# Attention weights times v: three fp32r products of split operands, or whole fp32 with each head on its own columns

## The chip, the cores and the metric

One Trainium2 chip, one of its NeuronCores. The metric is device time of one execution in microseconds (us); times of several runs are given by their median. TensorE (PE), VectorE (DVE), ScalarE (ACT), GpSimd (POOL) and the DMA queues (SP's above all) work side by side and meet at semaphores. The profile is of one execution, and its granted TensorE clock is shown as a share of 2.4 GHz.

## What is computed

Attention with a band and global tokens, then a token-shifted feed-forward layer ("Mix" in the kernel), then a routed layer of eight experts:

```python
k_all = np.concatenate([k_g, k_l], axis=2); v_all = np.concatenate([v_g, v_l], axis=2)
out_g = sm(scale * q_g @ k_all.T) @ v_all            # 32 global queries, 544 keys
mask = np.abs(pos[:, None] - pos[None, :]) <= 32
s_ll = np.where(mask, scale * q_l @ k_l.T, -1e9)     # 512 local queries
a_l = sm(np.concatenate([scale * q_l @ k_g.T, s_ll], axis=-1))
out_l = a_l @ np.concatenate([v_g, v_l], axis=2)
x = concat([out_g, out_l])                           # 4 x 544 x 512
x = _moe_ref(x)                                      # Mix: relu(xk@w_k)^2 @ w_v * sigmoid(xr@w_r)
return _moe2_ref(x)                                  # one expert of 8 for each token
```

Batch 4, 8 heads of 64, all in fp32.

## The kernel before, in words

The program has two stages. Up to about 480 us attention and Mix are interleaved; behind that come the experts, which the change doesn't touch.

Attention is cut into 16 units, one for each pair of heads of each batch element (`divmod(u,4)`). In a unit there are four items of 128 local queries (`item`, L212) and one global item of 2 x 32 queries (`gitem`, L257). An item runs through: scores on PE (`twin`, L197, the two heads on the two halves of the array's rows), mask and minimum on DVE (L222), exp on ACT (L225), scaling on POOL (L231), four transposes on PE (L237), a copy out of PSUM (`split`, L106), the product with v on PE (L245), and the eviction into `xT` on ACT (L249, L250). `xT` holds the attention output, transposed, and is what Mix reads.

Units 0 to 3 are "early" (`NF=4`): their operands stay whole fp32. From unit 4 on each operand is split in a high part in fp32r and the rest, and a product is three: high x high, high x low, low x high (`parts`, L105). For the weights `split` does this with a copy on ACT (L118) and a subtraction on DVE (L120) into `ph` and `plo`; for v `prep_v` (L184) does it on POOL (L191, L193), from one staging tile `vn`, into two half tiles. An early unit reads v from one of the two tiles `ve` as it was loaded. The product for an item takes v as the stationary operand with both heads' 128 columns and the weights of both heads as 256 moving columns; two of the four 64 x 128 blocks of the result are used, and two evictions fetch them.

The order of work comes in two steps. Generators announce each piece with its engine, a duration in us and places of buffers (`op("P",.65,("av",),("ph",),...)`), and `Sched` (L42) runs them against clocks of its own, by priority; the tile framework's scheduler then orders the instructions on each engine by its own timing. Instruction order and DMA order therefore move when a duration or a place count changes. Loads are issued on SP's queue, in order: `load` (L121) for q and k, `load_v` (L134) for v, `weight` (L396) for the weights of Mix, which ACT, DVE and POOL turn into high and low parts (L423 is the last step of each).

Of the kernel before, what the change touches and what calls it, by code (L numbers as in the profile page):

```python
# [34 lines left out]
PP=(0,0,0,1,0,0,0,1); TW=(1,1,1,(2,4,6),3)  # L35
NR=4; NP=4
# [47 lines left out]
class Attn:  # L84


    def __init__(s,tc,ident,mask,q_l,k_l,v_l,q_g,k_g,v_g,xT,sb,ps):
# [4 lines left out]
        s.vn=sb.tile([P,4,2,P],F32,name="vn",bufs=1)
# [7 lines left out]
        s.V={}; s.nat=set(); s.vnat=set(); s.T={}; s.sdone={}; s.vdone={}; s.odone={}  # L100
    def places(s,t):
# [59 lines left out]
    def prep(s,u,name):  # L161
# [21 lines left out]
        s.T[u]["n"]+=1  # L183
    def prep_v(s,u):  # L184
        nc=s.nc; L=[]
        for hf in range(2):
            yield op("G",.59)
            v=s.sb.tile([P,2,2,2,P],F32R,tag=f"v{hf}",name=f"v{u}_{hf}",bufs=1)
            f=lambda a:a.rearrange("p i a c -> p (i a c)")
            i=f(s.vn[:,2*hf:2*hf+2])  # L190
# [21 lines left out]
    def item(s,u,i,S_,held):  # L212
# [34 lines left out]
        yield op("A",.33,(),("av",))  # L247
# [61 lines left out]
    def run(s,sched,units,may):  # L309
        for u in units:  # L310
# [12 lines left out]
    def run_v(s,units):
        for u in units[NF:]:
            yield wait(lambda: u in s.vnat and all(s.vdone.get(v,0)>=5 for v in range(u)))
            yield from s.prep_v(u)

# [784 lines left out]
```

## Time and profile before

| | us |
|---|---|
| median of 3 runs (757.11 to 761.41) | 759.85 |
| the profiled execution's own time | 762.52 |
| its span, first to last instruction | 760.8 |
| PE busy / DVE busy in the span | 707.8 / 481.9 |
| ACT busy / POOL busy in the span | 394.9 / 343.5 |

Busy time of PE is that of its matrix products, which overlap: one lasts about 0.28 us, and the next one can start 0.11 us behind it. So what a group of products costs is read from the starts on the timeline, and a mean duration isn't its price. PEld is the loading of weights, which runs beside the products. A whole fp32 product shows as two records, a transpose or an fp32r product as one. The timeline gives start and duration, engine, source line, tiles out<-in, then rows x columns of the array, partitions x elements of the moving operand, and how many instructions are merged in the row.

### The profile page before, as it was taken

What the parts mean: (1) busy time and instruction counts of PE and PEld (TensorE: products, weight loads), DVE (VectorE), ACT (ScalarE), POOL (GpSimd) and SP (SyncE); (2) the same over time, 40 slices, a digit from 0 to 9 for tenths busy, and PEclk for the clock granted to TensorE, in tenths of its full rate; (3) what the DMA queues carried; (4) which work ended last, traced back from release to release, by engine and by line L of the source; (5) the groups of instructions that cost most, each with busy time, mean ns of one, the idle gap of its engine ahead of it and who ended that gap; (6) DMA issues with size and microseconds to landing.
All of it is one profiled execution on the core that took longest, in us unless ns stands there. A gap on an engine that the chain in (4) does not pass through costs nothing. (4 is left out here: it accounts for less than half of the span.)

```text
span 760.8 us, 13892 instructions
## 1 busy us (share of the span) xinstructions
PE 707.8 (93%) x4702; PEld 606.1 (80%) x4702; DVE 481.9 (63%) x1393; ACT 394.9 (52%) x1038; POOL 343.5 (45%) x483
## 2 busy tenths in 40 slices
PE   4887998899999999999999899989879999999996
PEld 2565786698898988978888789877677999889795
DVE  6587689758697685795864865577844534434361
ACT  4698876754575653565654624324733514335251
POOL 6368858724655246562455262012733513413431
PEclk9899998999999999999999999999989999999999
DMA  6674144211302211202100320225964724606530
GB/s 154 174 223 129 33 121 119 54 30 35 81 17 55 57 23 38 68 22 58 35 21 29 118 104 2 64 103 180 301 226 149 242 85 129 203 26 190 170 126 22
DMA packets 93184, 76.36 MB, mean 100 GB/s; under 512 B 70350, under 2 KB 74446, under 8 KB 93074
## 3 DMA queue, kind: packets, MB, share of 16 engines
q1 hardware_dynamic: 89618, 64.27, 29.0%
q0 software_dynamic: 3456, 10.75, 4.0%
q8 instruction: 53, 0.87, 0.5%
q14 instruction: 57, 0.47, 0.2%
HBM read 66.08 MB, written 9.44 MB: 99 GB/s over the span
## 5 line engine op out<-in xcount | busy, mean ns | idle before, releaser
L231 POOL TENSOR_SCALAR pl<-pl,mx 128x192 f32<-128x192 f32 (+1 forms) x128 | 60.6, 488 | 91.4 <-DVE mx L228 68.8
L21 PE MATMUL psk<-xs,slot0h 128*128 128x256 f32 x256 | 73.4, 290 | 1.8 <-ACT xs L454 1.1
L23 PE MATMUL psk<-xs,slot0h 128*128 128x256 f32 x256 | 73.0, 286 | 0.7 <-POOL xs L456 0.7
L225 ACT ACTIVATE pl<-pl,mx 128x224 f32<-128x224 f32 (+1 forms) x128 | 58.6, 459 | 27.6 <-DVE mx L222 25.7
L24 PE MATMUL psk<-xs,slot0l 128*128 128x256 f32 x256 | 72.1, 282 | 0.0
L900 ACT ACTIVATE hh<-ph 128x256 fp32r<-128x256 f32 (+2 forms) x56 | 22.4, 399 | 78.8 <-PE ph L24 45.6
L456 POOL TENSOR_TENSOR xs<-xm,xs 128x512 fp32r<-128x512 f32 (+1 forms) x36 | 45.7, 1276 | 37.6 <-ACT xs L454 25.5
L449 POOL TENSOR_SCALAR xm<-xT,mut 128x256 f32<-128x256 f32 (+7 forms) x96 | 43.6, 469 | 28.9 <-DVE kl L469 13.1
L21 PE MATMUL psv<-slot1h,kh 128*128 128x512 f32 x136 | 54.9, 404 | 0.3 <-ACT slot1h L421 0.3
L23 PE MATMUL psv<-slot1l,kh 128*128 128x512 f32 x136 | 54.1, 398 | 0.4 <-POOL slot1l L423 0.4
L901 DVE SCALAR_TENSOR_TENSOR hl<-ph,hh 128x256 fp32r<-128x256 f32 (+2 forms) x56 | 24.7, 442 | 46.4 <-ACT hh L900 44.3
L24 PE MATMUL psv<-slot1h,kl 128*128 128x512 f32 x136 | 53.9, 396 | 0.0
L452 DVE SCALAR_TENSOR_TENSOR xm<-xT,mut,xm 128x256 f32<-128x256 f32 (+7 forms) x96 | 47.0, 525 | 6.8 <-POOL xm L449 6.7
L21 PEld LDWEIGHTS psk<-xs,slot0h 128*128 128x128 f32 x256 | 47.8, 189 | 2.8 <-ACT xs L454 1.4
L23 PEld LDWEIGHTS psk<-xs,slot0h 128*128 128x128 f32 x256 | 48.4, 189 | 1.2 <-POOL xs L456 0.9
L24 PEld LDWEIGHTS psk<-xs,slot0l 128*128 128x128 f32 x256 | 48.3, 189 | 0.3
L245 PE MATMUL av<-ph,v 128*128 128x256 f32 x192 | 44.5, 294 | 3.7 <-ACT xT L250 2.6
L872 POOL DMA_INDIRECT xs<-y,idx x23 | 26.7, 1162 | 45.0 <-PE pt L879 22.5
L120 DVE TENSOR_TENSOR plo<-ptp,ph 128x512 fp32r<-128x512 f32 x48 | 32.9, 685 | 18.0 <-ACT ph L118 17.8
L237 PE MATMUL ptp<-ident,pl 128*128 128x128 f32 x256 | 40.3, 283 | 3.2 <-POOL earlyl L176 2.2
L21 PE MATMUL ph<-xh,slot2h 128*128 128x256 f32 (+1 forms) x128 | 38.3, 299 | 5.2 <-issue 5.2
L245 PEld LDWEIGHTS av<-ph,v 128*128 128x128 f32 x192 | 33.2, 191 | 6.6 <-ACT xT L250 3.9
(550 smaller groups left out, 2359.6 us busy)
## 6 DMA issues: line engine op xcount, KB each, us to landing
st<-in_moe_w_dram SPq DMA_DIRECT2D x42, 512.0 KB, 3.9
sw<-in_moe_w_dram SPq DMA_DIRECT2D x22, 512.0 KB, 5.2
y<-r SPq DMA_DIRECT2D x17, 256.0 KB, 2.0
qn<-in_q_l_dram SPq DMA_DIRECT2D x32, 128.0 KB, 4.4
kn<-in_k_l_dram SPq DMA_DIRECT2D x32, 128.0 KB, 2.6
earlyh<-in_moe_w_k_dram SPq DMA_DIRECT2D x8, 512.0 KB
raw<-in_moe_w_v_dram SPq DMA_DIRECT2D x8, 512.0 KB
vn<-in_v_l_dram SPq DMA_DIRECT2D x24, 96.0 KB, 2.0
```

The lines of the kernel that those rows point to most:

```text
L21: i=nc.tensor.matmul(out,wh,xh,start=first,stop=False)
L23: nc.tensor.matmul(out,wh,xl,start=False,stop=False)
L24: return nc.tensor.matmul(out,wl,xh,start=False,stop=last)
L120: nc.vector.tensor_sub(out[1],x,out[0].bitcast(F32))
L225: nc.scalar.activation(p[:,h,ks],p[:,h,ks],AF.Exp,bias=mx[:,h:h+1],scale=-1.0,accum_out=mx[:,4+h:5+h])
L231: nc.gpsimd.tensor_scalar(out=p[:,h,ks],in0=p[:,h,ks],scalar1=mx[:,6+h:7+h],scalar2=0.0,op0=ALU.mult,op1=ALU.add)
L237: nc.tensor.transpose(pt[:,c,h],p[:,h,c*96:c*96+P],s.ident)
L245: nc.tensor.matmul(o,s.v(u,x,i,c),P_[y][:,c],start=c==m==0,stop=c==1 and m==len(parts)-1)
L449: nc.gpsimd.tensor_scalar(out=x[:,u,o:o+k],in0=s.xT[b][:,c,q:q+k],scalar1=m[:,1,c:c+1],scalar2=0.0,op0=ALU.mult,op1=ALU.add)
L452: nc.vector.scalar_tensor_tensor(out=x[:,u,o:o+k],in0=s.xT[b][:,c,1+q:1+q+k],scalar=m[:,0,c:c+1],in1=x[:,u,o:o+k],op0=ALU.mult,op1=ALU.add)
L456: nc.gpsimd.tensor_sub(xl[:,cs,:n],x[:,:,:n],xh[:,cs,:n].bitcast(F32))
L872: s.nc.gpsimd.indirect_dma_start(out=s.xs[i][:,j,:],out_offset=None,in_=s.y,in_offset=IndirectOffsetOnAxis(ap=s.idx[:,ch:ch+1],axis=0))
```

## The change

- Weights and v of all units are whole fp32. `split` has only the copy left for the weights, `prep_v`, `run_v` and the tile `vn` are gone, and the two tiles `ve` serve all units in turn: v of unit u is loaded when the products of unit u-2 are done.
- Each head has a product of its own. For an item the head's 64 columns of v are stationary, its 128 columns of weights move, and the result goes to its own 64 partitions of one PSUM tile, so 64 columns of the array each. That is two chunks x two heads, four products of 64 x 128, and one eviction of 128 x 128 instead of two of 64 x 128.
- For the global item the weights are stationary, 32 columns for each head, and the head's 64 columns of v move: five chunks x two heads, and two evictions instead of one.
- The durations of these pieces are new, `ph` has three buffers instead of two, `plo` is gone.

```diff
-        if s.early(u):
-            vn=s.ve[u%2]
-            yield op("Q",3.5,(),(),lambda: all(s.vdone.get(v,0)>=5 for v in range(u%2,u,2)))
-        else:
-            vn=s.vn
-            yield op("Q",3.5,("vn",))
-            if u==NF: nc.gpsimd.memset(vn,0.0)
+        vn=s.ve[u%2]
+        yield op("Q",3.5,(),(),lambda: all(s.vdone.get(v,0)>=5 for v in range(u%2,u,2)))
...
-    def prep_v(s,u):
-            nc.gpsimd.tensor_scalar(out=f(v[:,0]),in0=i,scalar1=1.0,scalar2=0.0,op0=ALU.mult,op1=ALU.add)
-            nc.gpsimd.tensor_sub(f(v[:,1]),i,f(v[:,0]).bitcast(F32))
...
-        P_=s.weights(u)
-        yield from s.split(u,EV[i],P_,pt.rearrange("p c h q -> p c (h q)"),"pt",(.48,.61))
-        yield op("P",.65 if len(parts)>1 else .87,("av",),("ph",),when=lambda: u in s.V)
-        o=s.ps.tile([P,512],F32,tag="av",name="av",bufs=1)[:,:256]
+        P_=s.weights()
+        yield from s.split(u,EV[i],[P_],pt.rearrange("p c h q -> p c (h q)"),"pt",(.48,.61))
+        yield op("P",.47,("av",),("ph",),when=lambda: u in s.V)
+        o=s.ps.tile([P,512],F32,tag="av",name="av",bufs=1)[:,:P]
         for c in range(2):
-            for m,(x,y) in enumerate(parts):
-                nc.tensor.matmul(o,s.v(u,x,i,c),P_[y][:,c],start=c==m==0,stop=c==1 and m==len(parts)-1)
+            for h in range(2):
+                r=slice(h*HD,(h+1)*HD)
+                nc.tensor.matmul(o[r],s.V[u][:,i,c,r],P_[:,c,h*P:(h+1)*P],start=c==0,stop=c==1)
...
-        nc.scalar.activation(x[0:64,pr,c0:c0+P],o[0:64,0:P],AF.Copy)
-        nc.scalar.activation(x[64:128,pr,c0:c0+P],o[64:128,P:2*P],AF.Copy)
+        nc.scalar.activation(x[:,pr,c0:c0+P],o,AF.Copy)
...
-        yield op("P",.85,("av",),("ph",),when=lambda: u in s.V)
+        yield op("P",.65,("av",),("ph",),when=lambda: u in s.V)
         for c in range(5):
-            cs=slice(c*64,(c+1)*64)
-            for m,(x,y_) in enumerate(parts):
-                nc.tensor.matmul(o,G[x][:,cs],s.v(u,y_,min(c,3),c//4),start=c==m==0,stop=c==4 and m==len(parts)-1)
+            for h in range(2):
+                q=slice(h*32,(h+1)*32)
+                nc.tensor.matmul(o[q],G[:,c*64+h*32:c*64+(h+1)*32],s.V[u][:,min(c,3),c//4,h*HD:(h+1)*HD],start=c==0,stop=c==4)
...
-    sched.add(a.run_v(units),1.5)
```

How this moves instructions, at three places. First PE, at an item of a late unit among the products of Mix (`psl`, `psk`, `psv`; `av` is the value product, `ptp` and `ptq` are transposes, `sga` and `sgb` the global item's scores, a row is one instruction with its output's partitions x columns). Before:

```order
L24 MATMUL psl<-rt,g_250 10x128
L245 MATMUL av<-ph,v_0_3920 128x256
L245 MATMUL av<-plo,v_0_3920 128x256
L245 MATMUL av<-ph,v_0_3920 128x256 x2
L245 MATMUL av<-plo,v_0_3920 128x256
L245 MATMUL av<-ph,v_0_3920 128x256
L237 MATMUL ptp<-ident,pl_115 128x128 x4
```

And after, at a place of the same kind:

```order
L24 MATMUL psv<-slot1h,kl 128x512
L21 MATMUL psv<-slot1h,kh 128x512
L227 MATMUL av<-ph,ve_107 64x128 x4
L242 MATMUL sga<-kw_4279,gT_4280 64x512 x3
L242 MATMUL sgb<-gT_4280 64x32 x3
L160 MATMUL ptq<-ident,qn_4314 128x128 x4
```

Six products over the whole array have become four over 64 columns each, back to back, with full-width work of Mix on either side.

Second POOL, where v of a late unit was split between the scaling of two items (`pl`) and the work on k (`kw`). Before:

```order
L176 TENSOR_SCALAR kw_1752<-gT_1753 128x8x32
L193 TENSOR_TENSOR v_1_1785<-vn,v_1_1785 128x512
L231 TENSOR_SCALAR pl_112<-pl_112,mx 128x192 x2
L231 TENSOR_SCALAR pl_113<-pl_113,mx 128x224 x2
L231 TENSOR_SCALAR pl_114<-pl_114,mx 128x224 x2
L231 TENSOR_SCALAR pl_115<-pl_115,mx 128x192 x2
L191 TENSOR_SCALAR v_0_2040<-vn 128x512
L193 TENSOR_TENSOR v_0_2040<-vn,v_0_2040 128x512
L191 TENSOR_SCALAR v_1_2075<-vn 128x512
L193 TENSOR_TENSOR v_1_2075<-vn,v_1_2075 128x512
```

And after:

```order
L212 TENSOR_SCALAR pl_111<-pl_111,mx 128x192 x2
L212 TENSOR_SCALAR pl_112<-pl_112,mx 128x224 x2
L399 TENSOR_TENSOR slot1l<-w,slot1h 128x512
L169 TENSOR_SCALAR kw_1663<-kw_1663 128x2x3x32 x2
L212 TENSOR_SCALAR pl_113<-pl_113,mx 128x224 x2
L212 TENSOR_SCALAR pl_114<-pl_114,mx 128x192 x2
```

The four steps on v for each late unit are gone from POOL's order; the rest stands as it did.

Third SP's queue in the early part, with what each issue waits for in brackets (DMAHW: a queue's own turn). Loads of `earlyh` are weights of Mix (`w_k`, then `w_r`), `qn`, `kn` and `gn` q, k and the global rows of a unit, `ve` is v. Before:

```order
L406 DMA earlyh<-in_moe_w_k_dram 128x4x256 [waits DMAHW5_49,DVE_49,Activation_49]
L127 DMA qn_417<-in_q_l_dram 128x4x64 [waits DMAHW6_49,PE_49]
L127 DMA qn_417<-in_q_l_dram 128x4x64 [waits DMAHW7_49]
L130 DMA gn<-in_q_g_dram 32x64 [waits DMAHW0_49,PE_49]
L130 DMA gn<-in_q_g_dram 32x64 [waits DMAHW1_49]
L131 DMA gn<-in_k_g_dram 32x2x64 [waits DMAHW2_49]
L146 DMA ve_108<-in_v_l_dram 96x64 [waits DMAHW3_49]
L146 DMA ve_108<-in_v_l_dram 96x64 [waits DMAHW4_49]
L406 DMA earlyh<-in_moe_w_k_dram 128x4x256 [waits DMAHW5_49,DVE_49,Activation_49]
L127 DMA kn_553<-in_k_l_dram 128x4x64 [waits DMAHW6_49,PE_49]
L127 DMA kn_553<-in_k_l_dram 128x4x64 [waits DMAHW7_49]
L406 DMA earlyh<-in_moe_w_k_dram 128x4x256 [waits DMAHW0_49,DVE_49,Activation_49]
```

And after (`qn_591` and `kn_623` belong to unit 4, as `kn_553` does above, and `ve_107` is v of unit 2):

```order
L141 DMA ve_107<-in_v_l_dram 32x4x64 [waits DMAHW2_49,PE_49]
L142 DMA ve_107<-in_v_l_dram 32x3x64 [waits DMAHW3_49]
L143 DMA ve_107<-in_v_g_dram 32x4x64 [waits DMAHW4_49]
L126 DMA qn_591<-in_q_l_dram 128x4x64 [waits DMAHW5_49]
L126 DMA qn_591<-in_q_l_dram 128x4x64 [waits DMAHW6_49]
L126 DMA kn_623<-in_k_l_dram 128x4x64 [waits DMAHW7_49]
L129 DMA gn<-in_q_g_dram 32x64 [waits DMAHW0_49]
L129 DMA gn<-in_q_g_dram 32x64 [waits DMAHW1_49]
L130 DMA gn<-in_k_g_dram 32x2x64 [waits DMAHW2_49]
L382 DMA earlyh<-in_moe_w_k_dram 128x4x256 [waits DMAHW3_49,DVE_49,Activation_49]
L382 DMA earlyh<-in_moe_w_k_dram 128x4x256 [waits DMAHW4_49,DVE_49,Activation_49]
L382 DMA earlyh<-in_moe_w_k_dram 128x4x256 [waits DMAHW5_49,DVE_49,Activation_49]
```

The last three loads of `w_k` stood between the loads of units 3, 2 and 4; now they stand together behind v of unit 2 and all of unit 4's q, k and global rows.

## Rows read from the trace of the kernel before

**Rows 1.** The page, part 1: busy us (share) xinstructions of each engine.
```profile
PE 707.8 (93%) x4702; PEld 606.1 (80%) x4702; DVE 481.9 (63%) x1393; ACT 394.9 (52%) x1038; POOL 343.5 (45%) x483
```

**Rows 2.** Busy time by stage: start:end us, PE, PEld, DVE, ACT, POOL, clock, DMA.
```profile
20.00:100.00 80.00, 69.24 (x433) 52.97 (x434) 57.50 (x191) 63.13 (x209) 53.56 (x82) 0.94 0.51 135
100.00:160.00 60.00, 51.34 (x345) 42.07 (x343) 47.29 (x118) 40.19 (x117) 40.93 (x50) 0.94 0.33 92
160.00:440.00 280.00, 275.36 (x2110) 244.58 (x2109) 204.54 (x717) 160.60 (x486) 130.10 (x215) 1.00 0.18 48
```

**Rows 3.** Timeline of PE: a late global item's products, and a late item's.
```profile
249.43 0.22 PE L290 MATMUL avg<-v,plo 128*64 128x128 f32 x1
...
250.22 0.40 PE L237 MATMUL ptp<-ident,pl 128*128 128x128 f32 x2
...
252.82 0.28 PE L245 MATMUL av<-ph,v 128*128 128x256 f32 x1
...
253.52 0.39 PE L264 MATMUL sga<-kw,gT 128*64 128x512 f32 x1
```

**Rows 4.** Timeline of PE: an early item's products and what follows.
```profile
58.21 1.13 PE L245 MATMUL av<-ph,ve 128*128 128x256 f32 x4 [0.21 <-ACT xT L250]
59.18 0.25 PE L157 MATMUL pgt<-ident,gn 96*128 96x96 f32 x1
```

**Rows 5.** Timeline of PE: an early global item; row three is a narrower window.
```profile
30.58 0.66 PE L167 MATMUL ptq<-ident,kn 128*128 128x128 f32 x4
31.17 1.31 PE L290 MATMUL avg<-ve,ph 128*64 128x128 f32 x10
...
31.98 0.49 PE L290 MATMUL avg<-ve,ph 128*64 128x128 f32 x3
32.41 0.33 PE L167 MATMUL ptq<-ident,qn 128*128 128x128 f32 x1
```

**Rows 6.** Timeline of PE: early scores, the two heads on the array's row halves.
```profile
56.12 0.51 PE L208 MATMUL s__795<-earlyl 64*128 64x192 f32 x2
56.38 0.32 PE L208 MATMUL s__796<-earlyl 64*128 64x192 f32 x1
56.47 0.35 PE L208 MATMUL s__795<-earlyl 64*128 64x224 f32 x1
56.54 0.54 PE L208 MATMUL s__796<-earlyl 64*128 64x224 f32 x2
```

**Rows 7.** Timeline of PE: fp32r products with 64 columns, then full width.
```profile
226.67 0.29 PE L264 MATMUL sgb<-gT 128*64 128x32 f32 x3
226.82 0.37 PE L245 MATMUL av<-ph,v 128*128 128x256 f32 x1
```

**Rows 8.** Groups by line: busy us, mean ns of one; idle before, releasers.
```profile
L120 DVE TENSOR_TENSOR plo<-ptp,ph 128x512 fp32r<-128x512 f32 x48 | 32.9, 685 | 18.0 <-ACT ph L118 17.8
L193 POOL TENSOR_TENSOR v<-vn,v 128x512 fp32r<-128x512 f32 x24 | 32.4, 1351 | 1.1
...
L250 ACT ACTIVATE xT<-av 64x128 f32<-64x128 f32 x64 | 17.5, 273 | 0.8
...
L191 POOL TENSOR_SCALAR v<-vn 128x512 fp32r<-128x512 f32 x24 | 16.3, 678 | 31.7 <-PE av L245 30.8 <-PE pgt L157 0.9
```

**Rows 9.** Waits of PE from 20 to 160 us: total us, times, longest.
```profile
PE av L245 <- ACT xT L250: 3.6, 6, 1.5
...
PE avg L290 <- POOL v L193: 0.6, 1, 0.6
```

**Rows 10.** Timeline of POOL and of PE: last weight conversions, first long uses.
```profile
56.34 1.27 POOL L423 TENSOR_TENSOR slot0l<-w,slot0h 128x512 fp32r<-128x512 f32 x1
...
69.73 1.28 POOL L423 TENSOR_TENSOR wrl<-w,wrh 128x512 fp32r<-128x512 f32 x1
...
91.23 0.60 PE L21 MATMUL psk<-xs,slot0h 128*128 128x256 f32 x3
...
106.75 0.50 PE L21 MATMUL psr<-wrh,xs 128*128 128x512 f32 x1
```

More of the change, by code (lines that the diff above doesn't have):

```diff
@@ L35 @@
 PP=(0,0,0,1,0,0,0,1); TW=(1,1,1,(2,4,6),3)
-NR=4; NP=4
+NR=4; NP=4; NA=3
 FX=(3,5,7); WJ=(288,320,352); MW=352; FW=(2,4,6); NW=(2,3); NST=2
@@ L91, in __init__ @@
         s.gn=sb.tile([96,P],F32,name="gn",bufs=1)
-        s.vn=sb.tile([P,4,2,P],F32,name="vn",bufs=1)
         s.ve=[sb.tile([P,4,2,P],F32,tag=f"v{i}",name=f"ve{i}",bufs=1) for i in range(2)]
@@ L99, in __init__ @@
         nc.gpsimd.memset(s.pg,0.0); nc.gpsimd.memset(s.og,0.0)
-        s.V={}; s.nat=set(); s.vnat=set(); s.T={}; s.sdone={}; s.vdone={}; s.odone={}
+        s.V={}; s.nat=set(); s.T={}; s.sdone={}; s.vdone={}; s.odone={}
     def places(s,t):
@@ L108, in split @@
         nc=s.nc; r=(place,) if place else ()
-        if s.early(u):
+        if s.early(u) or len(out)==1:
             if engine=="A":
@@ L135, in load_v @@
         nc=s.nc; b,pr=divmod(u,4); h0=2*pr
-        if s.early(u):
-            vn=s.ve[u%2]
-            yield op("Q",3.5,(),(),lambda: all(s.vdone.get(v,0)>=5 for v in range(u%2,u,2)))
-        else:
-            vn=s.vn
-            yield op("Q",3.5,("vn",))
-            if u==NF: nc.gpsimd.memset(vn,0.0)
+        vn=s.ve[u%2]
+        yield op("Q",3.5,(),(),lambda: all(s.vdone.get(v,0)>=5 for v in range(u%2,u,2)))
         for j in range(2):
@@ L150, in load_v @@
         yield wait(None)
-        s.vnat.add(u)
-        if s.early(u): s.V[u]=[vn]
+        s.V[u]=vn
     def prep_g(s,u):
@@ L183, in prep @@
         s.T[u]["n"]+=1
-    def prep_v(s,u):
[L185 to L190, printed above, removed]
-            nc.gpsimd.tensor_scalar(out=f(v[:,0]),in0=i,scalar1=1.0,scalar2=0.0,op0=ALU.mult,op1=ALU.add)
-            yield op("G",1.23,(),("vn",) if hf else ())
-            nc.gpsimd.tensor_sub(f(v[:,1]),i,f(v[:,0]).bitcast(F32))
-            L.append(v)
-        s.V[u]=L
     def cols(s,i): return slice(32*(i==0),224-32*(i==3))
@@ L238, in item, with weights @@
         s.pt_.append(p)
-        P_=s.weights(u)
-        yield from s.split(u,EV[i],P_,pt.rearrange("p c h q -> p c (h q)"),"pt",(.48,.61))
-        yield op("P",.65 if len(parts)>1 else .87,("av",),("ph",),when=lambda: u in s.V)
-        o=s.ps.tile([P,512],F32,tag="av",name="av",bufs=1)[:,:256]
+        P_=s.weights()
+        yield from s.split(u,EV[i],[P_],pt.rearrange("p c h q -> p c (h q)"),"pt",(.48,.61))
+        yield op("P",.47,("av",),("ph",),when=lambda: u in s.V)
+        o=s.ps.tile([P,512],F32,tag="av",name="av",bufs=1)[:,:P]
         for c in range(2):
-            for m,(x,y) in enumerate(parts):
-                nc.tensor.matmul(o,s.v(u,x,i,c),P_[y][:,c],start=c==m==0,stop=c==1 and m==len(parts)-1)
+            for h in range(2):
+                r=slice(h*HD,(h+1)*HD)
+                nc.tensor.matmul(o[r],s.V[u][:,i,c,r],P_[:,c,h*P:(h+1)*P],start=c==0,stop=c==1)
         s.vdone[u]+=1
-        yield op("A",.33,(),("av",))
+        yield op("A",.2,(),("av",))
         x=s.xT[b]; c0=1+SG+i*P
-        nc.scalar.activation(x[0:64,pr,c0:c0+P],o[0:64,0:P],AF.Copy)
-        nc.scalar.activation(x[64:128,pr,c0:c0+P],o[64:128,P:2*P],AF.Copy)
+        nc.scalar.activation(x[:,pr,c0:c0+P],o,AF.Copy)
         yield wait(None)
         s.odone[u]+=1
-    def weights(s,u):
-        return [s.sb.tile([P,2,256],F32 if s.early(u) else F32R,tag=t,name=t,bufs=2) for t in ("ph","plo")[:2-s.early(u)]]
-    def v(s,u,w,i,c): return s.V[u][0][:,i,c] if s.early(u) else s.V[u][i//2][:,w,i%2,c]
+    def weights(s): return s.sb.tile([P,2,256],F32,tag="ph",name="ph",bufs=NA)
     def gitem(s,u):
@@ L282, in gitem @@
             nc.tensor.transpose(pt[:,c*64:c*64+P],s.pg[:,min(c*P,480):min(c*P,480)+P],s.ident)
-        G=[t.rearrange("p c q -> p (c q)")[:,:320] for t in s.weights(u)]
-        yield from s.split(u,EV["g"],G,pt[:,:320],"pt",(.32,.4))
-        yield op("P",.85,("av",),("ph",),when=lambda: u in s.V)
-        o=s.ps.tile([P,512],F32,tag="av",name="avg",bufs=1)[:64,:P]
+        G=s.weights().rearrange("p c q -> p (c q)")[:,:320]
+        yield from s.split(u,EV["g"],[G],pt[:,:320],"pt",(.32,.4))
+        yield op("P",.65,("av",),("ph",),when=lambda: u in s.V)
+        o=s.ps.tile([P,512],F32,tag="av",name="avg",bufs=1)[:64,:HD]
         for c in range(5):
-            cs=slice(c*64,(c+1)*64)
-            for m,(x,y_) in enumerate(parts):
-                nc.tensor.matmul(o,G[x][:,cs],s.v(u,y_,min(c,3),c//4),start=c==m==0,stop=c==4 and m==len(parts)-1)
+            for h in range(2):
+                q=slice(h*32,(h+1)*32)
+                nc.tensor.matmul(o[q],G[:,c*64+h*32:c*64+(h+1)*32],s.V[u][:,min(c,3),c//4,h*HD:(h+1)*HD],start=c==0,stop=c==4)
         s.vdone[u]+=1
-        yield op("A",.16,(),("av",))
-        nc.scalar.activation(s.og[:64],o,AF.Copy,scale=mx[:,7:8])
+        yield op("A",.32,(),("av",))
+        for h in range(2):
+            q=slice(h*32,(h+1)*32)
+            nc.scalar.activation(s.og[q,h*HD:(h+1)*HD],o[q],AF.Copy,scale=mx[q,7:8])
         yield op("P",.06,("av",))
@@ L322, in run @@
             sched.add(s.gitem(u),1)
[L323 to L326, printed above, removed]
 def band(nc,const):
@@ L723, in phase1 @@
     groups=[[0,1],[2,3],[4,5],[6,7],[8,9],[10,11],[12,13],[14,15],[16]]
-    sched=Sched(dict(s=2,pt=2,av=1,cm=3,p=NP,ph=2,xs=2,r=NR,raw=4,rawv=2,qn=1,kn=1,gn=1,vn=1,g=1,yT=2),dict(P=7.5,A=2.0,D=3.3,G=7.7,Q=0.7,W=0))
+    sched=Sched(dict(s=2,pt=2,av=1,cm=3,p=NP,ph=NA,xs=2,r=NR,raw=4,rawv=2,qn=1,kn=1,gn=1,g=1,yT=2),dict(P=7.5,A=2.0,D=3.3,G=7.7,Q=0.7,W=0))
     done=lambda b: all(a.odone.get(u,0)>=5 for u in range(4*b,4*b+4))
```

## The prediction

> **What bounds the kernel now.** The page's totals come first: TensorE is busy for 707.8 us, 93% of the span; no other engine passes 63% [rows 1]. The table by stage says where that share is real. The change touches attention alone, whose value products (L245, L290) end at 427 us. From 160 to 440 us PE is busy 275.4 of 280 us at the full granted clock (1.00, the 2.4 GHz level), DVE 204.5, POOL 130.1. From 20 to 160 us PE is busy 69.2 of 80 and 51.3 of 60, and DVE (47.3 of 60) and ACT (63.1 of 80) are near it [rows 2]. So a microsecond of TensorE is worth a whole one behind 160 us, and only part of one ahead of it. The third view is the timeline, for what a group of products costs from its start to the next group's: durations of single products overlap and can't be added.
>
> **Prices.** A late item (units 4 to 15) runs six fp32r products of 256 columns: 252.82 to 253.52, 0.70 us. Thirteen of the fifteen products of a late global item last from 249.43 to 250.22, so all take 0.91 [rows 3]. An early item (units 0 to 3, whole fp32) shows four records for two products, so whole fp32 goes through the array twice: 58.21 to 59.18, 0.97 us [rows 4]. The early global item is the nearest row to the new product, and has exactly its shape: whole fp32, 64 weight columns, 128 moving ones, two passes each. Ten passes start from 31.17; the eighth starts at 31.98, which is 0.05 for a bare first weight load and 0.109 a pass [rows 5].
>
> The same rows show a charge. The x4 row ends at 31.24 and a record lasts 0.27, so its last transpose started at 30.97; the 64-column group starts 0.20 later instead of 0.11. Its own last pass started near 32.21, and the next transposes follow at 32.41, again 0.20 later [rows 5]. Waiting 0.09 and loading the first weights bare (0.05) makes 0.14 us for each change of shape. The fp32r products with 64 weight columns do not pay this: behind the three short ones at 226.67 the next group starts at 226.82, 0.15 for three [rows 7]. The Trainium skill (TensorEngine Tiling (Array Packing), Key Properties) says that changing the tiling mode drains TensorE. The trace agrees for whole fp32 and differs for fp32r [rows 5, 7]; by the page's rule the late global items of before would pay already, the change would add some 24 changes fewer, and the result would be about 3 us lower. I go by the rows.
>
> **The change, part by part.**
>
> *Products.* An item now has four products of 64 x 128 in whole fp32, so eight passes; a global item ten of 32 x 64, twenty passes. If the two heads' column halves stream side by side, an item takes 4 x 0.109 = 0.44 us. The trace has no such pair of column halves. The nearest rows are the scores, where the heads lie on row halves: passes of both heads run interleaved there, s__796 at 56.38 and 56.54, s__795 between them at 56.47 and lasting to 56.82, each head at its own pace [rows 6]. I take full overlap; the other end is none, 0.87. A pass of 64 moving columns I estimate at half of 0.109, 0.055: a global item takes 0.55, without overlap 1.09. The Trainium skill (TensorE: Matmul & The Clock Gate, Part 3: Packing small matmuls) gives 2.38x for three column tiles, 0.79 of the ideal. No row here shows it; by it an item would take 0.56 and the forecast would rise by some 8 us, an estimate.
>
> *Changes of shape.* In the instruction order the array's shape (full, row halves, fp32 columns) changes 107 times in attention before, 236 after. Behind the 130th three-part product, near 126 us, it is 64 and 146: with two items and one global item that moved ahead, +87 for the same work; +42 ahead of it.
>
> *The bound part.* 44 late items and 11 global items: before 44 x 0.70 + 11 x 0.91 = 40.8 us; after 44 x 0.44 + 11 x 0.55 = 25.4; 87 changes x 0.14 = 12.2. Net **-3.2 us**, all on the path. Had I left the charge out, this would be -15.4.
>
> *The early part.* 16 early items x 0.97, 4 late x 0.70, 4 early global ones x 1.14, one late 0.91: 23.8 us; after 20 x 0.44 + 5 x 0.55 = 11.6 and 42 x 0.14 = 5.9: -6.3 of TensorE. TensorE idles for 19.4 of these 140 us [rows 2], so I count half, **-3.1**, with ends 0 and -6.3.
>
> *Other engines.* Gone are DVE's 48 + 12 subtractions (0.685 us each for the 48, 32.9 in all), POOL's two steps on v (16.3 + 32.4 us), and one of an item's two evictions on ACT (17.5) [rows 8]. Of the global item one DVE copy stays, and ACT evicts twice. Behind 160 us TensorE covers all this, and it counts nothing; if the cover went (TensorE shorter by 3 us), DVE would still have 70 us of slack. Ahead of 160 us a fourth of it falls, some 8 us of DVE net and 7 of ACT, where they share the limit; TensorE there waits 3.6 us for the eviction and 0.6 for v's split [rows 9]. Between 0 and -15 I take **-3**, near the waits, since a wait that goes leaves the next engine's. After it DVE's conversions of weights are late next.
>
> *Queues.* Loading v into two buffers waits for TensorE two units back, and the order puts the last three loads of wk behind v of unit 2 and all of unit 4's q and k on SP. The cover: wk's last conversion started at 56.34 and wr's at 69.73, and their first long uses come at 91.23 and 106.75 [rows 10]. I cost it at nothing; with that cover gone, each us late is one us on the early part.
>
> **Sum.** 3.2 + 3.1 + 3.0 = 9.3 us against the profiled execution's own 762.5: 753.2. The median of the runs is 2.7 lower (759.85), so I forecast **750.5**. Its own range: with all early savings, -3.2 - 6.3 - 10 of relief, 740; with 0.20 a change (the whole gap) and nothing early, 762.
>
> **Rivals.** 0.5% of 759.85 is 3.8 us, about what a measurement of this kernel can tell from no change: faster is below 756.05, slower above 763.65.
>
> - *The halves run one after the other* (slower). Place: each value product on TensorE. Price: 44 x 0.43 + 11 x 0.55 = 25 us behind 126 us, and half of 20 x 0.43 + 5 x 0.55, 5.7, ahead: 750.5 + 30.7 = 781. It decides once about a third of the overlap is lost (9.3 of 30.7). For it: no row shows two column halves at once, and both stream all 128 rows, which row halves do not. Against: row halves do overlap, in whole fp32 too [rows 6]. 0.16.
> - *The relief is hidden anyway.* Ahead of 160 us transfers and the other engines set the pace, and only the -3.2 stays: 756.6. For it: the early waits are spread over many releasers. 0.15.
> - *The changes of shape cost nothing*, as with fp32r [rows 7]: 87 x 0.14 + half of 42 x 0.14 = 15.1 more, 735. Against it are the fp32 rows themselves [rows 5]. 0.07.
> - *Weights come late*: loads queued behind v hold the first long products by some 8 us: 758.5. Against: 33 us of cover [rows 10]. 0.08.
>
> That the change doesn't do what it says I exclude: the order shows the four products of an item back to back, and no step on v on POOL. The forecast keeps 0.50; 0.04 is for an order that goes badly elsewhere.
>
> **How the numbers follow.** Faster: 0.44 of the forecast, 0.07 of free changes, half of the hidden relief, 0.02 of late weights: 0.60. Same: 0.06 + 0.07 + 0.05 = 0.18. Slower: the serial rival, the bad order and the tails, 0.22. The range 738 to 768 leaves out the serial case and the lower half of free changes, some 2 in 10.
>
> **What would show it.** Right: in the new profile the two heads' value products start as pairs, an item lasts 0.44 us plus 0.05, and 0.20 stands between the last product ahead of it and its first, and again behind it; PE still busy 98% from 160 us on. Wrong: passes of the two heads 0.109 apart one after another (serial); a group that follows its neighbour at 0.11 (free changes); psk starting clearly behind 91 us (late weights); DVE or ACT ending most of TensorE's waits behind 160 us.

## The result, and the profile after

The change takes the median from 760.49 us (20 runs, 756.73 to 762.64) to **753.65 us** (20 runs, 747.65 to 757.50): ratio 0.9903, 95% interval 0.9885 to 0.9921. The forecast was 750.5. The profiled execution took 750.19 us (span 748.3), 12.3 less than that of before. Medians are of all runs; in the experiments the ratios leave out three runs that lie over 1.5% above the fastest of their kernel.

The page's totals, to be read beside [rows 1]: every engine has less to do, TensorE by 6.8 us, DVE by 35.9, POOL by 48.1.

```profile
PE 701.0 (94%) x4962; PEld 585.6 (78%) x4962; DVE 446.0 (60%) x1345; ACT 375.4 (50%) x978; POOL 295.4 (39%) x434
```

The table by stage, with the columns of [rows 2]:

```profile
20.00:100.00 80.00, 67.61 (x533) 50.71 (x535) 53.09 (x189) 58.76 (x199) 48.62 (x77) 0.87 0.51 136
100.00:160.00 60.00, 56.80 (x463) 45.76 (x458) 44.42 (x120) 43.56 (x129) 34.62 (x46) 0.94 0.37 103
160.00:440.00 280.00, 274.52 (x2194) 231.68 (x2193) 180.50 (x670) 146.16 (x433) 102.49 (x185) 0.99 0.18 49
```

Behind 160 us TensorE is still busy 98% of the time. The new thing is the granted clock (third number from the end): 0.87, 0.94 and 0.99, where before it was 0.94, 0.94 and 1.00. In the rows below the level is either full or half (2.4 or 1.2 GHz), so a stretch of length L with a mean of c spent 2 x (1 - c) x L at half. Between 20 and 440 us that makes 9.6 + 7.2 + 0 = 16.8 us before and 20.8 + 7.2 + 5.6 = 33.6 us after.

The timeline of PE answers [rows 3 to 5]: a late item, a narrower window at its start, a late global item with its neighbours, and a late item with products of Mix on both sides.

```profile
249.55 0.25 PE L150 MATMUL pgt<-ident,gn 96*128 96x96 f32 x1
249.73 0.66 PE L227 MATMUL av<-ph,ve 128*64 128x128 f32 x8
250.32 0.33 PE L545 MATMUL pslt<-ident,lt 128*128 128x128 f32 x1
...
249.73 0.33 PE L227 MATMUL av<-ph,ve 128*64 128x128 f32 x2
...
241.90 0.75 PE L268 MATMUL avg<-ve,ph 128*32 128x64 f32 x20
242.58 0.55 PE L218 MATMUL ptp<-ident,pl 128*128 128x128 f32 x3
...
404.64 0.28 PE L21 MATMUL psk<-xs,slot0h 128*128 128x256 f32 x1
404.85 0.66 PE L227 MATMUL av<-ph,ve 128*64 128x128 f32 x8
405.44 0.39 PE L23 MATMUL psk<-xs,slot0h 128*128 128x256 f32 x1
405.66 0.28 PE L24 MATMUL psk<-xs,slot0l 128*128 128x256 f32 x1
405.78 0.28 PE L21 MATMUL psk<-xs,slot0h 128*128 128x256 f32 x1
```

In a window of 0.03 us two passes start: the two heads' column halves do run side by side. The eight passes start as four pairs, at 0, 0.16, 0.27 and 0.38 us (read in still narrower windows), and the next group follows 0.20 behind the last pair: 0.59 us from start to start. The twenty passes of the global item take 0.68. Among products of Mix, which stand 0.12 apart (405.66 to 405.78), the item starts 0.21 behind its neighbour, and the second product behind it comes 0.22 after the first: so 0.09 ahead and 0.10 behind belong to the item too. Where transposes follow, as behind the global item, the part behind is 0.06 instead of 0.10.

The conversions of weights and first long uses [rows 10], here of POOL, then of PE, and two waits of PE between 20 and 160 us (total, times, longest) [rows 9]:

```profile
65.46 1.72 POOL L399 TENSOR_TENSOR slot0l<-w,slot0h 128x512 fp32r<-128x512 f32 x1 [0.60 <-ACT slot0h L397]
...
87.92 1.26 POOL L399 TENSOR_TENSOR wrl<-w,wrh 128x512 fp32r<-128x512 f32 x1 [0.40 <-ACT wrh L397]
...
94.24 0.39 PE L21 MATMUL psk<-xs,slot0h 128*128 128x256 f32 x1
...
110.44 0.39 PE L21 MATMUL psr<-wrh,xs 128*128 128x512 f32 x1
...
PE s__947 L189 <- ACT pg L252: 2.1, 1, 2.1
...
PE av L227 <- ACT xT L231: 1.6, 2, 1.1
```

The last conversions come 9 and 18 us later than before, the long products 3 and 4 us later. The eviction makes PE wait 1.6 us instead of 3.6; the wait for ACT's exponentials of a global item (pg) ends at 66.1 us.

Five stretches of the changed kernel, with the same columns as the table by stage, and a wait between 160 and 440 us, show two places where the clock falls:

```profile
61.00:66.00 5.00, 1.50 (x13) 1.00 (x13) 4.19 (x14) 3.33 (x12) 4.29 (x6) 0.94 0.93 318
66.00:82.00 16.00, 15.91 (x69) 12.68 (x70) 13.36 (x34) 9.86 (x34) 12.90 (x15) 0.50 0.38 128
...
408.00:413.60 5.60, 3.38 (x46) 2.52 (x45) 5.18 (x30) 1.66 (x6) 0.83 (x2) 1.00 0.41 126
413.60:420.40 6.80, 5.90 (x27) 5.55 (x28) 6.67 (x16) 4.96 (x11) 3.42 (x2) 0.50 0.54 208
420.40:426.00 5.60, 5.60 (x49) 5.60 (x49) 4.20 (x5) 3.08 (x5) 2.88 (x2) 1.00 0.69 238
...
PE psL L662 <- DVE acc L630: 1.6, 1, 1.6
```

PE has little to do from 61 to 66 us, and then runs 16 us at half level, busy throughout. At 411 us it waits 1.6 us for one small DVE result (psL, which starts at 412.87), and soon behind it 6.8 us are at half level. The same products show it on the timeline, 0.21 us apart at half level and 0.12 at full:

```profile
418.03 0.41 PE L24 MATMUL psk<-xs,slot0l 128*128 128x256 f32 x1
418.24 0.41 PE L21 MATMUL psk<-xs,slot0h 128*128 128x256 f32 x1
...
420.75 0.28 PE L24 MATMUL psk<-xs,slot0l 128*128 128x256 f32 x1
420.87 0.28 PE L21 MATMUL psk<-xs,slot0h 128*128 128x256 f32 x1
```

A single wait isn't enough, though. The longest wait between 160 and 440 us in the same trace, 2.4 us up to 315.39 us, also stands among products of Mix back to back, and the clock stays at 1.00:

```profile
PE psr L577 <- DVE fe L571: 3.0, 2, 2.4
...
308.00:325.00 17.00, 14.64 (x135) 13.28 (x134) 13.79 (x63) 11.42 (x40) 5.89 (x12) 1.00 0.05 12
```

The runs follow the clock too. Over the 20 runs of the changed kernel the mean granted clock lies between 0.959 and 0.977, the time follows it (correlation -0.85, 490 us per unit of clock), and the middle is 0.968. No run of the 20 has a higher clock than the profiled execution, 0.977, so its profile shows less of the clock's loss than the usual run has. Nineteen runs of the kernel before, beside the first experiments, have 0.984 in the mean.

### The profile page after: what moved, and what is told of

Same layout as the page of the kernel before. It is cut to its first block, busy times and chain, and to the rows that moved or that the text cites. A ratio compares the mean times of both kernels' runs of the same rounds, so it can differ in the third digit from the quotient of the medians.

```text
span 748.3 us, 14229 instructions
## 1 busy us (share of the span) xinstructions
PE 701.0 (94%) x4962; PEld 585.6 (78%) x4962; DVE 446.0 (60%) x1345; ACT 375.4 (50%) x978; POOL 295.4 (39%) x434
## 5 line engine op out<-in xcount | busy, mean ns | idle before, releaser
L23 PE MATMUL psk<-xs,slot0h 128*128 128x256 f32 x256 | 75.8, 297 | 0.0
L21 PE MATMUL psk<-xs,slot0h 128*128 128x256 f32 x256 | 74.9, 298 | 0.3 <-ACT xs L430 0.3
L24 PE MATMUL psk<-xs,slot0l 128*128 128x256 f32 x256 | 74.9, 293 | 0.0
L206 ACT ACTIVATE pl<-pl,mx 128x224 f32<-128x224 f32 (+1 forms) x128 | 58.5, 459 | 20.6 <-DVE mx L203 19.8
L425 POOL TENSOR_SCALAR xm<-xT,mut 128x256 f32<-128x256 f32 (+6 forms) x96 | 44.2, 476 | 46.4 <-DVE xT L280 21.1
L23 PEld LDWEIGHTS psk<-xs,slot0h 128*128 128x128 f32 x256 | 50.3, 196 | 1.2 <-issue 0.9
L24 PEld LDWEIGHTS psk<-xs,slot0l 128*128 128x128 f32 x256 | 50.2, 196 | 1.1 <-issue 0.7
L21 PEld LDWEIGHTS psk<-xs,slot0h 128*128 128x128 f32 x256 | 49.9, 198 | 1.3 <-ACT xs L430 0.4
L227 PE MATMUL av<-ph,ve 128*64 128x128 f32 x512 | 43.9, 294 | 4.0 <-DVE xT L280 2.1
L428 DVE SCALAR_TENSOR_TENSOR xm<-xT,mut,xm 128x256 f32<-128x256 f32 (+6 forms) x96 | 41.5, 466 | 8.5 <-POOL xm L425 8.3
L218 PE MATMUL ptp<-ident,pl 128*128 128x128 f32 x256 | 43.3, 292 | 2.3 <-ACT ph L111 1.1
L111 ACT ACTIVATE ph<-ptp 128x512 f32<-128x512 f32 x64 | 37.7, 591 | 10.5 <-PE ptp L218 10.2
L227 PEld LDWEIGHTS av<-ph,ve 128*64 128x64 f32 x512 | 27.9, 141 | 18.1 <-issue 8.1
```

The costliest lines, as they stand in the source:

```text
L21: i=nc.tensor.matmul(out,wh,xh,start=first,stop=False)
L23: nc.tensor.matmul(out,wh,xl,start=False,stop=False)
L24: return nc.tensor.matmul(out,wl,xh,start=False,stop=last)
L206: nc.scalar.activation(p[:,h,ks],p[:,h,ks],AF.Exp,bias=mx[:,h:h+1],scale=-1.0,accum_out=mx[:,4+h:5+h])
L218: nc.tensor.transpose(pt[:,c,h],p[:,h,c*96:c*96+P],s.ident)
L227: nc.tensor.matmul(o[r],s.V[u][:,i,c,r],P_[:,c,h*P:(h+1)*P],start=c==0,stop=c==1)
```

## The experiments

Ratios are to the kernel before, run on the same chip in the same hour. The changed kernel's is 0.9903, so 0.001 is 0.76 us.

**1. Full width.** Items on the full array in whole fp32, both heads' weights moving, as early units did before; no shape change for items.

```diff
-            for h in range(2):
-                r=slice(h*HD,(h+1)*HD)
-                nc.tensor.matmul(o[r],s.V[u][:,i,c,r],P_[:,c,h*P:(h+1)*P],start=c==0,stop=c==1)
+            nc.tensor.matmul(o,s.V[u][:,i,c],P_[:,c],start=c==0,stop=c==1)
...
-        nc.scalar.activation(x[:,pr,c0:c0+P],o,AF.Copy)
+        nc.scalar.activation(x[0:64,pr,c0:c0+P],o[0:64,0:P],AF.Copy)
+        nc.scalar.activation(x[64:128,pr,c0:c0+P],o[64:128,P:2*P],AF.Copy)
```

> The items' value products in whole fp32 over the full array again (two products of 128 x 256 for an item, two evictions), everything else as changed. Shape changes of the array in attention: 126 instead of 236. Theory (halves overlap, each change of shape costs 0.14 us): behind 126 us 42 items x (0.89 - 0.44) = +18.9 us and 71 changes fewer = -9.9; half of +9.9 - 5.5 ahead of it: 753.7 + 11 = 765 us. Rival (changes of shape cost nothing on the path): +18.9 + 5 = 778 us. Rival (the gain of the change comes from the other engines, not from the products): 754 us.

Measured 755.39 us, ratio 0.9928 (0.9901 to 0.9956), only 1.9 us above the changed kernel, at a clock of 0.981, and the intervals of the two overlap. So the last rival's 754 us comes out, and the theory is 10 us off. The item on the timeline costs 0.86 us (220.73 to 221.59) with no gap of 0.20:

```profile
220.62 0.27 PE L160 MATMUL ptq<-ident,kn 128*128 128x128 f32 x1
220.73 1.03 PE L225 MATMUL av<-ph,ve 128*128 128x256 f32 x4
221.59 0.38 PE L160 MATMUL ptq<-ident,kn 128*128 128x128 f32 x2
```

That is 0.08 to 0.12 more than 0.74 to 0.78 for the halves with what they cost their neighbours, 5 to 8 us for 64 items. The clock, 0.981 against 0.968, gives back 6.4 us at 490 us per unit, an estimate. This run therefore doesn't prove that the halves gain nothing; it does show that most of the 6.8 us can be had without them.

**2. Serial heads.** Both heads on the same 64 columns.

```diff
-        o=s.ps.tile([P,512],F32,tag="av",name="av",bufs=1)[:,:P]
+        o=s.ps.tile([P,512],F32,tag="av",name="av",bufs=1)[:HD,:2*P]
...
-                nc.tensor.matmul(o[r],s.V[u][:,i,c,r],P_[:,c,h*P:(h+1)*P],start=c==0,stop=c==1)
+                nc.tensor.matmul(o[:,h*P:(h+1)*P],s.V[u][:,i,c,r],P_[:,c,h*P:(h+1)*P],start=c==0,stop=c==1)
```

> The changed kernel with both heads' value products of an item on the same 64 columns of the array (each head's result on partitions 0 to 63, in its own half of the PSUM tile, two evictions), so that they must run one behind the other. Global items stay as they are. Theory (column halves stream side by side, and that is where the saving on the products comes from): an item's eight passes take 0.87 instead of 0.44 us; about 40 items behind 126 us x 0.43 = 17, and half of 24 x 0.43 = 5 ahead of it: 22 us slower than the changed kernel, 776 us, slower than the kernel before. Rival (the overlap is not worth anything, another limit holds the item at its time): 753 to 755.

Measured 771.26 us, ratio 1.0117 (1.0088 to 1.0145): 16 us above the changed kernel, nearest to the theory, which had said 22.

```profile
228.26 0.39 PE L23 MATMUL psr<-wrl,xs 128*128 128x512 f32 x1
228.58 1.09 PE L227 MATMUL av<-ph,ve 128*64 128x128 f32 x8
229.60 0.66 PE L160 MATMUL ptq<-ident,qn 128*128 128x128 f32 x4
```

Now the item takes 1.02 us (228.58 to 229.60), 0.43 more than 0.59, which is four passes of 0.109. Full width and serial heads stream equally long, and both evict twice; by the instruction order the serial kernel has 233 changes of shape, the full-width one 126. Their difference, 0.0189 or 14.4 us at about one clock (0.984 and 0.982), makes **0.13 us a change**, near the 0.14 of the forecast. (The two differ in the order of work too, and what that can do, in 7, is nearly as much as this difference.)

**3. The relief alone.** The kernel before without the two subtractions, and with zero tiles in their place, so this computes without the low parts of v and of the weights while PE's work stays.

```diff
-        nc.vector.tensor_sub(out[1],x,out[0].bitcast(F32))
+        if low: nc.vector.tensor_sub(out[1],x,out[0].bitcast(F32))
...
-            nc.gpsimd.tensor_sub(f(v[:,1]),i,f(v[:,0]).bitcast(F32))
```

> The kernel before, with the subtractions that make the low parts of v (POOL, 32.4 us) and of the weights (DVE, 38.8 us) left out; the low operands are tiles of zeros, so all products of TensorE stay and the output lacks the low parts. Theory (relief of the other engines is worth 3 us, ahead of 160 us): 757.5 us. Rival (relief is hidden): 760.5 us. Rival (relief is the main gain): 753 us or less.

Measured 759.25 us, ratio 0.9972 (0.9950 to 0.9994), 2.1 us faster: between the theory and the first rival, and only the second rival is out. The clock fell here too, with TensorE's work unchanged: 9.6 + 10.8 + 5.6 = 26 us at half level in the profile against 16.8. Up to Mix's last product (it starts at 503.6 us here, at 504.2 before) the two profiled executions differ by only 0.6 us.

```profile
20.00:100.00 80.00, 69.10 (x419) 52.82 (x420) 53.47 (x180) 61.97 (x202) 47.51 (x76) 0.94 0.52 136
100.00:160.00 60.00, 52.45 (x364) 44.77 (x363) 43.34 (x117) 42.90 (x130) 38.33 (x51) 0.91 0.33 91
160.00:440.00 280.00, 274.75 (x2116) 244.76 (x2113) 171.96 (x668) 160.77 (x485) 103.66 (x196) 0.99 0.17 46
```

**4. The order of loads.** The changed kernel with all of wk first (`N0=3` to `N0=8`), and with v behind the weights:

```diff
-    sched.add(a.loads_v(units),-1)
+    sched.add(a.loads_v(units[:2]),-1); sched.add(a.loads_v(units[2:]),1.6)
```

> The changed kernel with all eight loads of wk ahead of the loads of q, k and v in priority (N0=8 instead of 3). In the changed kernel wk's last conversion ended at 67 us instead of 58. Theory (covered: first long uses come behind 90 us): 753.7 us, within 1.5. Rival (the late weights cost what the block of psk came later, about 4.8 us): 749 us; the first psk then comes before 70 us and TensorE's clock does not fall near 65 us.

Measured 757.53 us, ratio 0.9950 (0.9927 to 0.9974). Mixing starts early, at 64.6 us, but gains nothing by it: neither expectation. The clock doesn't fall near 65 us here, but it falls earlier, and all of 17 to 41 us is at half level:

```profile
17.00:41.00 24.00, 14.76 (x66) 10.46 (x67) 20.50 (x49) 15.28 (x44) 21.97 (x22) 0.50 0.82 197
```

> The changed kernel with the loads of v from unit 2 on below the weights in the order (priority 1.6 in place of -1), so that on SP the last three loads of wk stand ahead of v of unit 2 again, as before the change. Theory (late weights leave TensorE idle at 61 to 66 us, and its clock then stays at the half level for 17 us): the idle stretch goes, mixing products start some 5 us earlier, the mean granted clock rises from 0.968 to about 0.98, and 0.012 times the 490 us per unit of clock that the changed kernel's own runs show is 6 us: 746 to 748 us. Rival (the loads' order is not what delays them, or the clock falls elsewhere): 752 to 756 us at a clock of 0.97.

Measured 761.50 us, ratio 1.0001 (0.9976 to 1.0026), clock 0.963. Theory and rival both fall short, the theory by more: wk's last conversion starts at 58.5 us, 7 us ahead of the changed kernel's, and the clock is lower still. In neither order do earlier weights gain anything. What late weights cost by themselves isn't shown, since each edit moved the rest of the order as well.

**5. Fewer changes of shape.** Two neighbouring items' products in one group, with one 256-column eviction and four buffers for the weights; then the fourth buffer alone (`NA=3` to `NA=4`).

```diff
+        pair[i]=P_
+        if len(pair)<2: return
+        yield op("P",.91,("av",),("ph","ph"),when=lambda: u in s.V)
...
+        for k in range(2):
...
+                    nc.tensor.matmul(o[r,k*P:(k+1)*P],s.V[u][:,i0+k,c,r],pair[i0+k][:,c,h*P:(h+1)*P],start=c==0,stop=c==1)
```

> The changed kernel with the value products of two neighbouring items in one group, one eviction of 256 columns for both, and four buffers for the weights. Shape changes 180 instead of 236 (108 instead of 146 behind 126 us). Theory (0.14 us for each change on the path): 38 x 0.14 = -5.3 and half of 18 x 0.14 = -1.3: 747 us. Rival (changes cost nothing on the path): 753.7 us. Rival (the first item's weights and scores wait for the second, and TensorE with them): 757 us or more.

Measured **739.90 us**, ratio 0.9712 (0.9678 to 0.9746), 7 us below the theory.

> The changed kernel with four buffers for the weights instead of three (the change that the pairs also needed), nothing else. Theory (the pairs won by fewer changes of shape and evictions): no difference beyond a reordering, 751 to 756 us. Rival (the fourth buffer won it, since exponentials and transposes can run further ahead): 745 us or less.

Measured 748.61 us, ratio 0.9813 (0.9779 to 0.9847), between the two. From there the pairs gain 0.0101, 7.7 us, for 48 changes fewer (180, not 228): 0.16 each with the saved evictions, if the two orders are otherwise alike, which no run shows.

```profile
214.79 0.28 PE L23 MATMUL psk<-xs,slot0h 128*128 128x256 f32 x1
214.91 0.28 PE L24 MATMUL psk<-xs,slot0l 128*128 128x256 f32 x1
215.12 1.09 PE L233 MATMUL av<-ph,ve 128*64 128x128 f32 x16
216.15 0.66 PE L219 MATMUL ptp<-ident,pl 128*128 128x128 f32 x4
```

A pair takes 1.03 us, 0.52 an item instead of 0.59; the product ahead of it stands 0.21 before it, where two of its own kind stand 0.12 apart.

**6. On from the pairs.** With v behind the weights, with a fifth buffer, and with all four items of a unit in a group (six buffers, `if len(pair)<4: return`, one 512-column eviction).

> The pairs of two items (739.9 us) with the loads of v behind the weights as in the run ahead. Theory (late weights): the idle stretches at 52 to 68 us and the half level from 67 to 81 us shrink, 733 to 737 us. Rival (order of the loads is not it): 739 to 742 us. By order it has 11 changes of shape more behind the 130th long product than the pairs had, which is 1 us against it.

Measured 743.38 us, ratio 0.9763 (0.9733 to 0.9792): not the theory, as with single items, and a little above the rival.

> The pairs with five buffers for the weights instead of four; 176 changes of shape. Theory (changes of shape; a fifth buffer has nobody who waits for it): 739 to 741 us, as the pairs. Rival (room for attention to run ahead is what wins): below 737.

Measured 744.52 us, ratio 0.9754 (0.9722 to 0.9785): neither, since both expected a gain or none.

> All four items of a unit in one group of 16 value products with one 512-column eviction (pairs had two items), six buffers for the weights. By order 151 changes of shape instead of the pairs' 180 and the changed kernel's 236. Theory (each change costs about 0.12 us, the 0.094 that a neighbour is late plus half of the 0.05 bare load of a group): 29 x 0.12 = 3.5 us below the pairs, 736 us. Rival (buffers and evictions won it, not the changes): 739 to 741; and if four items that wait for each other hold up the next unit, above 742.

Measured **738.59 us**, ratio 0.9683 (0.9656 to 0.9710), the lowest of all; its interval overlaps that of the pairs, so of the theory's 3.5 us only 1.3 (by the medians) or 2.2 (by the ratios) are seen, and not for certain. The scheduler sets other products between the parts of some groups; where one stays whole, four items take 1.89 us, 0.47 each:

```profile
240.00 1.97 PE L233 MATMUL av<-ph,ve 128*64 128x128 f32 x32
241.89 0.33 PE L219 MATMUL ptp<-ident,pl 128*128 128x128 f32 x1
```

**7. The early items, and the order alone.** 64 columns only for units 4 to 15, first with the planner told of the longer early products, then without.

```diff
-        yield op("P",.47,("av",),("ph",),when=lambda: u in s.V)
+        yield op("P",.87 if s.early(u) else .47,("av",),("ph",),when=lambda: u in s.V)
...
+            if s.early(u): nc.tensor.matmul(o,s.V[u][:,i,c],P_[:,c],start=c==0,stop=c==1)
...
-        yield op("A",.2,(),("av",))
+        yield op("A",.33 if s.early(u) else .2,(),("av",))
```

> The changed kernel with 64-column products only for the items of units 4 to 15; those of units 0 to 3 are on the full array, 256 columns wide, as they were before the change. TensorE then has more work ahead of 126 us (16 x 0.53 = 8.5 us, less 36 changes of shape x 0.12 = 4.3), where it idles, and the same work behind. Theory (the shorter products ahead of 126 us leave TensorE idle, which costs the clock; the mean granted clock falls from 0.984 to 0.968 with the change): clock back to 0.98, 0.012 x 490 = 6 us gained, some 2 lost: 748 to 751 us. Rival (the clock falls whatever the early products are, or the early saving counts): 754 to 758 at a clock of 0.97.

Measured 766.00 us, ratio 1.0050 (1.0027 to 1.0072), clock 0.969: outside both. The second kernel has the same products and evictions, and leaves out the two lines on durations:

> The run ahead's work (64-column products only for the items of units 4 to 15) with the planner's durations left as in the changed kernel (0.47 us for an item's products and 0.2 for its eviction in place of 0.87 and 0.33 for units 0 to 3), so that only the order of the work differs from the run that took 766.0 us. Theory (the 766 us came from the order: it puts waits of about 2 us for the routing at 319 and 420 us into the part that TensorE bounds, each with 7 to 10 us at the half clock behind it): 748 to 756 us, clock 0.97 to 0.98. Rival (full-width products ahead of 126 us cost it): 762 to 767 us.

Measured 752.39 us, ratio 0.9893 (0.9872 to 0.9913), clock 0.98, as the theory had it. So **the order alone is worth 0.0157, 11.9 us**. And this kernel, whose early items are back at full width, is as fast as the changed one (0.9903): what the halves save in the early items isn't seen in the time. The stages of the first, then of the second:

```profile
20.00:100.00 80.00, 64.56 (x438) 47.76 (x440) 58.23 (x180) 63.79 (x203) 53.66 (x76) 0.92 0.54 149
100.00:160.00 60.00, 54.77 (x438) 44.09 (x435) 38.38 (x124) 40.59 (x126) 34.22 (x47) 0.91 0.29 79
160.00:440.00 280.00, 273.82 (x2202) 230.83 (x2199) 173.31 (x652) 146.43 (x439) 93.29 (x177) 0.97 0.19 50
```

```profile
20.00:100.00 80.00, 68.30 (x497) 52.11 (x498) 54.55 (x192) 67.37 (x223) 47.80 (x77) 0.97 0.54 144
100.00:160.00 60.00, 56.07 (x468) 44.31 (x466) 42.69 (x118) 41.90 (x123) 35.12 (x46) 1.00 0.32 93
160.00:440.00 280.00, 273.66 (x2169) 230.84 (x2168) 179.92 (x675) 146.07 (x431) 103.88 (x185) 0.98 0.18 49
```

At half level the first spends 12.8 + 10.8 + 16.8 = 40.4 us, the second 4.8 + 0 + 11.2 = 16.0. Half of the difference is work not done, 12.2 us; the profiled spans differ by 11.7 (762.0 and 750.3). The Trainium skill (TensorE: Matmul & The Clock Gate, Terms) prices time at the low level the same way, as that time times the share of the clock that is missing; these two executions agree. Over all runs of the two kernels the mean clocks are 0.969 and 0.979, which by the same price is some 7 of the 12 us, an estimate. In the first kernel the stretch that TensorE bounds has such a fall of its own:

```profile
316.00:322.00 6.00, 4.59 (x39) 4.22 (x38) 5.36 (x27) 4.25 (x15) 3.22 (x7) 1.00 0.32 71
322.00:329.00 7.00, 7.00 (x34) 6.29 (x34) 2.80 (x9) 1.82 (x7) 1.82 (x5) 0.52 0.00 0
...
PE ptg L265 <- ACT pg L257: 1.4, 1, 1.4
```

One wait of 1.4 us, for ACT's exponentials of a global item and not for the routing, then 7 us at half level with PE busy throughout.

## Why the prediction was right, and where it was not

- **Products.** Right: the column halves overlap entirely (0.109 us from pair to pair, and serial heads cost 0.43 an item more). The Trainium skill (TensorE: Matmul & The Clock Gate, Part 3: Packing small matmuls) has 2.38x for three column tiles, by which the text had set 0.56 us against 0.44; with two halves this trace gives 2.0, so that loss does not show here. The global item's 64-column passes are 0.055 apart, as estimated.
- **Changes of shape.** Right in kind, and a little small in size. The gap of 0.20 (0.15 behind passes of 0.055) stands behind each group, the neighbour ahead is late by 0.09, and the 0.05 of a bare load comes once a group. The text missed one part: the second product behind the group is late by another 0.06 to 0.10. An item costs 0.59 + 0.09 + 0.06 to 0.10 = 0.74 to 0.78 us, so against the 0.70 of the one row that the text had priced, the charge takes back all that the halves give. With the part that was missed a change costs 0.15 to 0.17; the runs put it at 0.13 to 0.16, each from two kernels that differ in order too.
- **The bound part, -3.2.** Right in size, with two errors that offset each other: the charge was too small, and so was the price before. From the point where 390 of Mix's long products are done (212.8 us before, 205.0 after) both traces, counted in order, have the same work left, 32 items and 8 global items among it. In that stretch an item before takes 0.83 in the mean (26.4 us from start to next start for all 32), since many take 0.75 to 0.90 and four that wait 1.0 to 1.7; after, 18.9 us, 0.59 each. From there to Mix's last product (it starts at 504.2 us before and 493.7 after) it is 291.4 us before and 288.7 after: -2.7, although 6.8 us of it are at half level, up to 3.4 us of work. With the fourth buffer alone (experiment 5) it is 281.9, none of it at half level.
- **The early part, -3.1, half of -6.3.** By those prices 16 x (0.74 - 0.97) + 4 x (0.74 - 0.70) + 4 x (0.83 - 1.39) + (0.83 - 0.91) = -5.8 of TensorE, where 0.83 is 0.68 + 0.09 + 0.06 and 1.39 the 1.24 from start to start of [rows 5] with the same two charges. How much of it lay on the path can't be told apart from the next two points; with the early items back at full width (752.39 us) their part of it isn't missed.
- **Other engines, -3.** Leaving out the subtractions alone gave -2.1, beside the -3 for all of the relief. That kernel's clock fell too, so the relief may be worth more at an even clock. But the place was not as forecast: of the 5.0 us by which its profiled span is shorter, 0.6 lie ahead of Mix's last product.
- **Queues, 0.** The weights did come later, by 9 and 18 us, and the long products by 3 and 4. The cover was read too large: the first products with wk's weights (psk) start at 67.3 us before and not at 91.23, some 10 us behind the last conversion, and at 72.5 after, 5 us behind it. Still, bringing the weights forward, in two ways, gained nothing. PE's idle stretch up to 66 us ends with attention's own wait for ACT (pg, 2.1 us), not with weights.
- **What the sum lacked: a term for the clock.** It stood in [rows 2] (0.94 and 0.94), and was taken as given. In the profiled executions 16.8 us more are at half level between 20 and 440 us, up to 8.4 us of work; by the slope of the runs, 0.984 to 0.968 is 7.8 us, an estimate. Why the clock fell isn't shown. TensorE doesn't idle longer from 20 to 160 us than before (15.6 us against 19.4, with more of its busy time at half level). Kernels that give it more early work mostly have the higher clock (0.98 in experiments 1 and 2 and in the last one), but the one at 766.0 us has 0.969 with the same work as the last.
- **How near the forecast came is partly luck.** In the profiled executions the 12.5 us of span divide so: 7.8 ahead of the point with 390 long products, where 6.1 had been forecast for the early part and the relief and 0.9 for the 12 late items that lie ahead of it; 2.7 from there to Mix's last product; and 2.0 in the experts, which the change doesn't touch. There the execution before has a fall of its own (0.50 from 555.5 to 562.2 us), and the changed one has none. The median run gains only 6.8 us, at a lower clock than the profiled one. So 750.5 against 753.65 is a larger saving, of which the clock takes back a part that the text had not seen.
- **Rivals.** The halves don't run serially. Made serial, an item costs the 0.43 us more that the rival had priced; for the items that is 18.9 + 4.3 = 23 us, and 16 were measured, at a clock 0.016 higher than the changed kernel's. Free changes of shape are excluded by the gaps on the timeline. "Relief hidden" is not: 2.1 us is all that is seen of it.

What stays open: how much of the 6.8 us is the change and how much is the luck of its order. Kernels of the same products differ by 12 us by order alone, and every edit here moves it, the fourth and fifth buffers included. What doesn't hang on it are the prices read from starts on the timeline. No run here has column halves in fp32r; groups of 64 columns in fp32r pay no charge [rows 7].

## What to carry to other kernels

Two heads of 64 columns stream at once in whole fp32, but a group that small pays about as much for changing the array's shape as it saves; put several groups back to back before you count the gain (738.6 to 744.5 us in four kernels with two or four items in a group, 748.6 to 761.5 in four with one, of which only the fastest has the fourth buffer too). Where TensorE is the bound, look at the granted clock by stage before and after: a wait of 1.4 to 1.6 us in such a stretch can cost half of the 7 us that follow as well, though one of 2.4 us cost nothing more. And compare two orders of the same work before you read a difference of 1% as the effect of an edit.

## What was not expected of the hardware

- A wait of 1.4 or 1.6 us behind a full stretch was followed by 7 us at the 1.2 GHz level, with PE busy through nearly all of it, and a wait of 2.4 us in the changed kernel was not.
- Two orders of the same products differ by 12 us. In the two profiled executions half of the time at the low level accounts for it, over all runs for some 7 us.
- In whole fp32 the charge for a 64-column group falls on both neighbours: the group behind stands 0.20 us off instead of 0.11, the product ahead 0.21 instead of 0.12, and the second product behind comes 0.06 to 0.10 late. Full-width whole fp32 products pay none of it (0.11 ahead, experiment 1).
